# Batch 3's attention and token mixing two steps earlier in the first pair's second product

## The chip, the cores and the metric

The kernel runs on one core of a Trainium2 chip. The metric is the device time of one execution in microseconds (us). The engines are TensorE (PE, matmuls; PEld is its weight load), VectorE (DVE), ScalarE (ACT), GpSimd (POOL) and SyncE (SP, here only an issuer of DMAs). Each engine works through its own queue in order.

## The reference

Eight batches of attention (16 query heads, 4 key heads, 384 positions, 64 wide), followed by one ResMLP block over a model width of 1024:

```python
attn = softmax(q @ k.T / 8)                       # k, v repeated for groups of 4 query heads
x    = (attn @ v), heads side by side             # 8 x 384 x 1024
a1   = alpha1 * x + beta1
tok  = einsum('ts,bsd->btd', w_tok, a1)           # mixes the 384 positions
u    = x + lam * tok
a2   = alpha2 * u + beta2
ch   = maximum(a2 @ w_ch1, 0) @ w_ch2             # 1024 -> 4096 -> 1024
out  = u + lam * ch
```

## The kernel before

The two large products of the MLP set the pace. The batches are taken in four pairs. For each pair both products are done at once in a scheme with seven block products in place of eight, so that sums and differences of operands (`opb`, `tb`) and of weights (`w1`, and `w2` as blocks "11", "12", "21", "22") are formed on DVE beforehand. The first product of a pair gives the hidden layer, the second its output. While the products of one pair run, the attention and the token mixing of the next pair are done in between ("side work").

All five engines run in the order in which the program issues instructions. That order is written by hand: a pair's product is a generator that yields after each step, and a table `plan` says what is issued after which step. In the first pair's second product (`second_product`) a step is four C matmuls of 128x512 (L752), and there are 21 turns of 16 matmuls, 84 steps (0 to 83). After every turn ACT copies the sum out of its bank (L764) and, for turns 12 to 17, DVE adds a base (L767). Halfway through a turn ACT copies a start value into the bank of the next turn (L744). There are two such banks.

The side work of a batch (`side`) has 8 pieces p, one for each two query heads:

- `scores3`: three times four matmuls of scores (L260), each followed by an exponential on ACT (L269). Four exponential tiles go round.
- `av` (L295): 18 matmuls against v; then on DVE the reciprocal (L300), the scaling into `xr` (L303) and alpha1 (L309). `xr` and alpha1 are both in SBUF in L309; L303 reads PSUM.
- `tok` (L324, L328): the token mixing on PE; on DVE u = x + tok (L331, reads PSUM) and times alpha2 (L334, both inputs in SBUF), which gives the a2 of the piece. Then the piece's u is stored by SP (`spill`, 192 KB).
- `turn` (L398): three transposing matmuls of a2; ACT copies them (L400) into the operand for the next pair. In batch 2 a DMA transposes instead.

Each scores matmul group, `av`, `tok` and `turn` takes the next of three PSUM banks in rotation (`three`), and PE waits until what was in the bank three takes ago has been read.

Beside this, DVE works off the weights for later pairs: `sum_w2` (L499, 128x2048 bf16 with both inputs in SBUF; the results go to DRAM by SP, `keep_w2`) and `last_w2`, which is `sum_w2` with o = 4 at steps 61, 64, 68 and 71 for c = 0 to 3, and which frees a weight slot, so that POOL may issue the next load (`load_w1`, L183). From step 68 on a list `later` is flushed: POOL multiplies six finished tiles by lam (`scaled`, L790) and adds them to the output by DMA (L442).

At the end of the 84 steps come `sum_w1` (steps 77, 79 and 81, L510 and L515) and `sums_a` (L447 to L450), the sums of the next pair's operands. sums_a(j) needs the pieces j and j + 4 of batch 2 and j of batch 3. Then the next pair's first product begins (X, Y, Z at L831).

Batch 2's side work starts at step 0; its last pieces are `av` 7 at step 35 and `tok` 6 and 7 at steps 36 and 39. Batch 3's own table is shifted by 38.

Of the kernel before, what the change touches and what calls it, by code (L numbers as in the profile page):

```python
# [13 lines left out]
def kernel(  # L14
# [81 lines left out]
    turn, a2_turn = [0], [0]  # L96
# [117 lines left out]
    def side(b):  # L214
# [176 lines left out]
        def by_pe(p):  # L391
            return b in (0, 3) or b % 2 and p >= NP - (4 if first else 3)
# [14 lines left out]
        def put(k, *m):  # L407
            at.setdefault(k, []).append(m)
# [3 lines left out]
        for p in range(NP):  # L412
            put((4, 10, 14, 18, 24, 29, 33, 35)[p], av, p)
            put((8, 15, 17, 22, 27, 32, 36, 38 if b % 2 else 39)[p], tok_flip, p)
            if by_pe(p):
                put(((13, 20, 22, 28, 34, 37, 40, 42) if b == 3 else (0, 0, 0, 0, 0, 36, 39, 41))[p], turn, p)
        return at

    def loads(b):
# [147 lines left out]
    def free_blocks(side, gp):  # L567
        for kind in (side + "1", side + "2"):
            if (kind, gp) in block_slot:
                free(block_slot.pop((kind, gp)))  # L570
# [376 lines left out]
    with tc.manual_schedule(engines=order):  # L947
# [123 lines left out]
        def put(ps, phase, at, *m):  # L1071
            plan.setdefault((ps, phase, at), []).append(m)

        def put_all(ps, phase, table, at=lambda u: u):
            for u, ms in table.items():
                for m in ms:
                    put(ps, phase, at(u), *m)

        def put_flips(ps, phase, b, places):
            for u, m in zip(places, ((flip_k, b), *((flip_q, b, i, 2) for i in range(0, NP, 2)))):  # L1080
                put(ps, phase, u, *m)
# [30 lines left out]
        for ps in range(NB - 1):  # L1112
            c = 2 * ps + 2
            for i in range(9):
                put(ps, 0, (4, 8, 12, 16, 20, 24, 54, 58, 62)[i] if ps == 0 else 4 + 7 * i, load_next, c, 1)
                put(ps, 0, 70 + 3 * i if ps == 0 else 91 + 2 * i, load_next, c + 1, 1)
            put_flips(ps, 0, c, (44, 46, 50, 54, 58) if ps == 0 else range(76, 86, 2))
            put_all(ps, 1, side(c))
            for u, f, h in zip((8, 14, 14, 27, 32, 33) if ps == 0 else (10, 17, 18, 28, 33, 33),
                               (flip_q, flip_k, flip_q, flip_q, flip_k, flip_q), (0, 0, 2, 4, 2, 6)):  # L1120
                put(ps, 1, u, f, c + 1, h, 2)
            put_all(ps, 1, side(c + 1), lambda u: u + 38)
            for j, u in ((0, 77), (2, 80), (3, 83)) if ps == 0 else ((0, 76), (2, 79), (3, 81)):
                put(ps, 1, u, sums_a, j, 1 if j else 2)

        def steps(ps):
# [87 lines left out]
```

## Time and profile before

| what | value |
| --- | --- |
| three runs | 731.71, 734.32, 740.37 us; median 734.32 |
| the profiled execution | 731.92 us |
| its span | 729.9 us |
| PE busy | 717.4 us (98%) |
| DVE busy | 543.9 us (75%) |
| ACT busy | 373.8 us (51%) |
| POOL busy | 199.2 us (27%) |
| first pair's second product, first matmul to the next product's first | 128.1 to 234.4 us |

The span is the time between the first and the last instruction of the profiled execution; the execution's own time has 2.0 us more around it. A busy share is an average over the whole span. In the timelines a line gives the start in us from the span's start, the length in us, engine, line of the program, operation, output <- inputs, and how many instructions were merged; in brackets stands the idle time of the engine before it and what ended that.

### The profile page before, as it was taken

The page shows a single profiled execution, that of the slowest core. Times are in us where ns is not written, and L with a number is a line of the kernel's source. Part 1 is how long each engine was busy: PE and PEld are TensorE (multiplying, and loading weights), DVE is VectorE, ACT ScalarE, POOL GpSimd, SP SyncE. Part 2 cuts the span into 40 slices and gives each one's busy share as a digit, 9 for nine tenths or more (in the row PEclk, how much of TensorE's full clock was granted, in tenths as well). Part 3 has the DMA queues.
Part 4 walks back from the last instruction along what each step waited for, and adds up shares of the span by engine and source line. Part 5 has one row for each costly group of instructions (what it writes and reads, how often), then busy time and mean ns, then how long its engine had stood idle before and what let it go on. Part 6 is the DMA issues. An engine that isn't in the chain of part 4 may idle for free.

```text
span 729.9 us, 14511 instructions
## 1 busy us (share of the span) xinstructions
PE 717.4 (98%) x5716; PEld 408.7 (56%) x5716; DVE 543.9 (75%) x1009; ACT 373.8 (51%) x566; POOL 199.2 (27%) x242
## 2 busy tenths in 40 slices
PE   8899999999999999999999999999999999999998
PEld 4665555555555666555555566655555566654444
DVE  7888876577888988649678888748868988763354
ACT  7877666544563666643433466663333366650000
POOL 8844233221046551201022344200002222000011
PEclk9999999999999999999999999999999999999999
DMA  9999999999999999969989999998989999937965
GB/s 164 180 239 231 190 195 227 226 242 235 366 312 232 179 182 196 234 221 207 272 193 220 160 162 194 212 227 201 270 233 183 210 126 146 165 123 264 302 174 104
DMA packets 197616, 153.26 MB, mean 210 GB/s; under 512 B 90540, under 2 KB 175892, under 8 KB 197292
## 3 DMA queue, kind: packets, MB, share of 16 engines
q0 software_dynamic: 109872, 64.47, 65.4%
q1 hardware_dynamic: 86988, 87.42, 42.8%
q8 instruction: 44, 0.72, 0.4%
q10 hardware_dynamic: 688, 0.46, 0.2%
q14 instruction: 24, 0.20, 0.1%
HBM read 155.23 MB, written 39.85 MB: 267 GB/s over the span
## 4 chain that ended last, share of the span: by engine, by line
PE 90%; DVE 4%; POOL 2%; DMA 1%; issue 1%; ACT 1%; DVEq 0%; ACTq 0%; POOLq 0%
PE C L897 30%; PE X L831 17%; PE C L752 10%; PE Y L831 9%; PE Z L831 4%; PE sc L260 4%; PE X L681 4%; PE sc L295 3%; PE sc L324 3%; PE Y L681 3%; DMA ops<-obuf 1%; DVE pad L565 1%; PE Z L681 1%; PE tok L324 1%; POOL obuf L334 0%
## 5 line engine op out<-in xcount | busy, mean ns | idle before, releaser
L897 PE MATMUL C<-w,arena 128*128 128x512 bf16 (+2 forms) x744 | 168.3, 372 | 0.0
L269 ACT ACTIVATE es<-sc 128x1024 bf16<-128x1024 f32 x108 | 104.1, 1024 | 116.0 <-PE sc L260 107.6
L897 PEld LDWEIGHTS <-arena 128*128 128x128 bf16 x1040 | 94.8, 98 | 100.5 <-issue 5.1
L442 POOL DMA_DIRECT2D out_dram<-hT x45 | 40.0, 888 | 294.7 <-DVE hT L790 135.9
L836 ACT ACTIVATE hT<-X,bias 128x384 f32<-128x384 f32 x144 | 83.6, 582 | 60.0 <-PE X L831 55.2
L831 PEld LDWEIGHTS <-w 128*128 128x128 bf16 x768 | 75.1, 98 | 50.0
L831 PEld LDWEIGHTS <-pad 128*128 128x128 bf16 x576 | 56.4, 98 | 37.2
L183 POOL DMA_DIRECT2D w<-in_moe_w_ch_dram x48 | 45.4, 1002 | 105.6 <-PE X L831 36.5
L831 PE MATMUL X<-ops,w 128*128 128x384 bf16 x384 | 70.3, 326 | 0.0
L831 PE MATMUL X<-ops,pad 128*128 128x384 bf16 x384 | 70.3, 326 | 0.0
L897 PE MATMUL C<-pad,arena 128*128 128x512 bf16 (+2 forms) x296 | 70.2, 373 | 0.0
L324 PEld LDWEIGHTS <-wtokT 128*128 128x128 bf16 x576 | 39.0, 98 | 16.4 <-issue 3.4
L752 PEld LDWEIGHTS <-arena 128*128 128x128 bf16 x336 | 29.8, 98 | 30.0 <-issue 2.5
L331 DVE TENSOR_TENSOR xr<-sc,xr 128x384 f32<-128x384 f32 x48 | 26.5, 553 | 25.6 <-PE sc L324 14.3
L752 PE MATMUL C<-w,arena 128*128 128x512 bf16 x168 | 41.2, 379 | 0.0
L838 DVE TENSOR_TENSOR arena<-Y,hT 128x384 bf16<-128x384 f32 x48 | 26.5, 556 | 17.7 <-ACT hT L836 16.0
L295 PEld LDWEIGHTS <-es 128*128 128x128 bf16 x864 | 32.8, 97 | 11.3
L831 PE MATMUL Y<-ops,w 128*128 128x384 bf16 x192 | 39.1, 326 | 0.0
L831 PE MATMUL Z<-ops,w 128*128 128x384 bf16 x192 | 39.0, 326 | 0.0
L269 ACT ACTIVATE hT<-sc 128x1024 bf16<-128x1024 f32 x36 | 35.8, 1031 | 4.3 <-PE sc L260 4.0
L260 PE MATMUL sc<-qT,kT 64*128 64x384 bf16 (+2 forms) x504 | 37.2, 271 | 0.5 <-ACT hT L269 0.2
L842 ACT ACTIVATE arena<-X,bias 128x384 bf16<-128x384 f32 x48 | 27.9, 582 | 17.7 <-PE X L831 16.1
(190 smaller groups left out, 1175.1 us busy)
## 6 DMA issues: line engine op xcount, KB each, us to landing
w<-w2s SPq DMA_DIRECT2D x67, 512.0 KB, 5.1
w<-in_moe_w_ch_dram POOLq DMA_DIRECT2D x65, 512.0 KB, 9.8
pad<-w2s SPq DMA_DIRECT2D x25, 512.0 KB, 6.9
out_dram<-hT POOLq DMA_DIRECT2D x45, 256.0 KB, 7.1
out_dram<-xr SPq DMA_DIRECT2D x48, 192.0 KB, 5.3
q_raw<-in_q_dram POOLq DMA_DIRECT2D x28, 192.0 KB, 9.5
w2s<-w SPq DMA_DIRECT2D x10, 512.0 KB, 7.6
arena<-in_moe_w_ch_dram POOLq DMA_DIRECT2D x8, 512.0 KB, 15.9
```

What stands on the lines that cost most here:

```text
L183: nc.gpsimd.dma_start(out=w1[:, w1_slots[c]], in_=w1src[:, :, c * CW * P:(c + 1) * CW * P])
L260: nc.tensor.matmul(out=sc[:, hh, k % 4:k % 4 + n], lhsT=kT_[r, 2 * p // G, BLK[hh][sk], :], rhs=qT_[r, p, st:st + n, :], start=True, stop= ...
L269: nc.scalar.activation(out=e, in_=sc, func=EXP, scale=scale_qk)
L295: nc.tensor.matmul(out=av[:, hh, sq, :], lhsT=ess[k // 4][:, m % 2, k % 4, :], rhs=vb[:, sk, hk, :], start=(sk == 0), stop=(sk == NST - 1))
L324: nc.tensor.matmul(out=ps[:, tt, :], lhsT=wtokT[:, st, tt * P:(tt + 1) * P], rhs=a1s[p][:, st, :], start=(st == 0), stop=(st == NST - 1 an ...
L442: nc.gpsimd.dma_start(out=by_tok(out[b])[:, ms, dw * 512:(dw + 1) * 512], in_=o, accum_op=ADD)
L681: nc.tensor.matmul(out=ps[:, :n], lhsT=tb[G, o][:, dt, e * P:(e + 1) * P], rhs=opb(FIRST1[o], n)[:, dt], start=(o in (1, 2, 7) and dt == 0 ...
L752: nc.tensor.matmul(out=x, lhsT=lead_hid[:, t, FIRST2[o], ms * P:(ms + 1) * P], rhs=rhs[:, t % 4 * 512:(t % 4 + 1) * 512], start=(o in (1, ...
L831: nc.tensor.matmul(out=ps, lhsT=tb[g, o][:, dt, e * P:(e + 1) * P], rhs=opb(LEFT1[o])[:, dt], start=(o in (1, 2, 7) and dt == 0), stop=(dt ...
L836: nc.scalar.activation(out=snap[o, e], in_=ps, func=IDENT, bias=hi if o == 5 else lo)
L842: nc.scalar.activation(out=hid[:, t, 4], in_=ps, func=RELU, bias=hi)
L897: nc.tensor.matmul(out=x, lhsT=hid[:, t, LEFT2[o], ms * P:(ms + 1) * P], rhs=rhs[:, t % 4 * 512 + c0:t % 4 * 512 + c1], start=((not last o ...
```

## The change

It moves batch 3's whole side table from an offset of 38 to one of 36, for the first pair's second product alone (the later pairs keep 38). `turn` 2 of batch 3 goes from 22 to 23 in the table, so it moves from step 60 to 59, where all other pieces move by two. sums_a(0), for pieces 0 and 1, goes from step 77 to 76, ahead of the first sum_w1; sums_a(2) from 80 to 79; sums_a(3) from 83 to 81. The table of `turn` for batch 3 is not used elsewhere. No instruction is added or removed, and none has another shape.

```diff
             if by_pe(p):
-                put(((13, 20, 22, 28, 34, 37, 40, 42) if b == 3 else (0, 0, 0, 0, 0, 36, 39, 41))[p], turn, p)
+                put(((13, 20, 23, 28, 34, 37, 40, 42) if b == 3 else (0, 0, 0, 0, 0, 36, 39, 41))[p], turn, p)
...
-            put_all(ps, 1, side(c + 1), lambda u: u + 38)
-            for j, u in ((0, 77), (2, 80), (3, 83)) if ps == 0 else ((0, 76), (2, 79), (3, 81)):
+            put_all(ps, 1, side(c + 1), lambda u: u + (36 if ps == 0 else 38))
+            for j, u in ((0, 76), (2, 79), (3, 81)) if ps == 0 else ((0, 76), (2, 79), (3, 81)):
                 put(ps, 1, u, sums_a, j, 1 if j else 2)
```

Batch 3's steps, before and after:

| piece | before | after |
| --- | --- | --- |
| scores3 0 to 5 | 38, 44, 50, 59, 64, 69 | 36, 42, 48, 57, 62, 67 |
| av 0 to 7 | 42, 48, 52, 56, 62, 67, 71, 73 | 40, 46, 50, 54, 60, 65, 69, 71 |
| tok 0 to 7 | 46, 53, 55, 60, 65, 70, 74, 76 | 44, 51, 53, 58, 63, 68, 72, 74 |
| turn 0 to 7 | 51, 58, 60, 66, 72, 75, 78, 80 | 49, 56, 59, 64, 70, 73, 76, 78 |

## The prediction

> **What bounds the kernel now.** I read the page first, then windows of each engine's busy time over the first pair's second product, then the timelines of that stretch.
>
> The page: TensorE (PE) is busy for nearly all of the span.
>
> ```profile
> span 729.9 us, 14511 instructions
> PE 717.4 (98%) x5716; PEld 408.7 (56%) x5716; DVE 543.9 (75%) x1009; ACT 373.8 (51%) x566; POOL 199.2 (27%) x242
> ```
>
> The change removes no matmul, so it can win only idle time of PE. The windows show where that lies in the second product (127.9 to 234.5 us):
>
> ```profile
> 168.40:204.00 35.60, 35.60 (x348) 20.14 (x347) 27.69 (x44) 20.12 (x29) 0.91 (x1) 1.00 1.08 313
> 204.00:212.80 8.80, 8.21 (x82) 4.79 (x81) 7.64 (x12) 5.92 (x8) 1.76 (x2) 1.00 1.16 321
> 212.80:226.80 14.00, 12.81 (x138) 7.50 (x137) 12.65 (x16) 6.93 (x12) 12.44 (x11) 1.00 1.23 253
> ```
>
> Columns: stretch and its length, then PE, weight loads, DVE, ACT, POOL busy, granted clock (1.00), DMA share, GB/s. PE lacks 8.80 - 8.21 = 0.59 us in the second row and 14.00 - 12.81 = 1.19 us in the third, 1.78 us in all. That is 0.24% of the run: the most that can be won here. PE's timeline names the three places, in brackets at the line's end:
>
> ```profile
> 204.89 0.33 PE L324 MATMUL sc<-a,wtokT 128*128 128x128 bf16 x3 [0.59 <-ACT es L269]
> ...
> 221.20 0.33 PE L398 MATMUL sc<-ident,obuf 128*128 128x128 bf16 x3 [0.24 <-ACT es L269]
> ...
> 224.76 0.34 PE L324 MATMUL sc<-a,wtokT 128*128 128x128 bf16 x3 [0.95 <-DVE a L309]
> ```
>
> By the plan these are batch 3's tok 3 (step 60), turn 4 (step 72) and tok 6 (step 74). The first two wait for a score bank that an exponential still reads, the third for its operand from VectorE (DVE). Why DVE is late then is in its timeline and POOL's:
>
> ```profile
> 220.26 0.69 DVE L767 TENSOR_TENSOR hT<-C,hT 128x512 f32<-128x512 f32 x1 [0.39 <-ACT hT L764]
> 220.87 2.02 DVE L499 TENSOR_TENSOR w<-w,pad 128x2048 bf16<-128x2048 bf16 x1
> ...
> 223.62 1.08 DVE L309 TENSOR_TENSOR a<-xr,vecs 128x384 bf16<-128x384 f32 x1
> ...
> 225.44 1.74 DVE L309 TENSOR_TENSOR a<-xr,vecs 128x384 bf16<-128x384 f32 x1
> ```
>
> ```profile
> 211.92 0.88 POOL L183 DMA_DIRECT2D w<-in_moe_w_ch_dram  x1 [2.38 <-DVE pad L499]
> 212.82 1.28 POOL L790 TENSOR_TENSOR hT<-hT,vecs 128x512 f32<-128x512 f32 x1
> ...
> 220.24 1.55 POOL L790 TENSOR_TENSOR hT<-hT,vecs 128x512 f32<-128x512 f32 x1
> ...
> 222.71 1.57 POOL L790 TENSOR_TENSOR hT<-hT,vecs 128x512 f32<-128x512 f32 x1
> ...
> 225.19 1.56 POOL L790 TENSOR_TENSOR hT<-hT,vecs 128x512 f32<-128x512 f32 x1
> ```
>
> L499 otherwise takes 1.22 us and L309 0.56. Each slow one ends one ordinary length after a POOL L790 ends: 220.24 + 1.55 = 221.79, and 2.02 - 1.22 after 220.87 is 221.67; 222.71 + 1.57 = 224.28, and L309 ends at 224.70; 225.19 + 1.56 = 226.75, and the other L309 ends at 227.18. L331 and L303, with one input in PSUM, keep their 0.56 us there. So a DVE operation with both inputs in SBUF stands still while POOL multiplies. POOL's six multiplications start when the issue at 211.92 is through, every 2.5 us; that issue waits for the L499 of last_w2(1).
>
> The Trainium skill (SBUF — State Buffer, "Who interferes with whom") says the same as a rule: a DVE instruction with two SBUF inputs and a GpSimd instruction that reads SBUF exclude each other for the whole instruction, whoever starts first. Read as shared speed instead (2.02 / 1.22 = 1.7 times slower), the two collisions at the L499 and the L309 of av 7 below would cost about 0.8 + 0.4 us, not 1.7, and the sum would be 0.5 us less; the ends above speak for the rule.
>
> **The change, part by part.** I walked the queues of PE, ACT, DVE and POOL from step 32 (167.5 us) in the new order. Each instruction starts at the end of the one before it or at its last release. The lengths, start to start, are rows of the timelines: four C matmuls 0.86 us (0.96 after scores), score trio 0.76, av 0.55, tok 0.67, turn 0.17 on PE; exponential 0.91, L764 and L744 0.5 each, L400 0.37 on ACT; L300 0.22, L303 0.60, L309 0.47, L331 0.60, L334 0.48, L767 0.61, L499 1.14 on DVE; L790 1.28 and 0.96 for its store on POOL. The old order, walked alike, ends the product 0.4 us late (234.97 for 234.54) and gives the three stalls as 0.78, 0.41 and 1.50 us for 0.59, 0.24 and 0.95. So the walk finds the stalls, and is up to 0.6 us too harsh.
>
> *Moved by two steps: all 8 av, 8 tok, 7 turns and 18 scores of batch 3.* Their own time stays: 0 us. Each tok also issues one 192 KB store on SP. SP was behind anyway: tok 0 ran at 186.1 us, its store was issued at 195.5. The stores of tok 0, 2 and 4 pass one weight store each (steps 45, 54, 64), nothing else; the store that the L499 at 204.10 waits 1.1 us for keeps what is ahead of it. No moved step issues on POOL. 0 us; if a pass does delay that L499, it costs at most what the L499 has waited, 1.1 us.
>
> *Stall one.* tok 3 is now at step 58, one step after its scores, and turn 2 at 59 takes the next bank: four C matmuls lie between the three bank users. The walk leaves 0.12 of 0.59 us: **-0.5** (-0.6 to 0).
>
> *New at step 36.* Batch 2's tok 6 and batch 3's first scores now meet. The third score needs tok 6's own bank, free after its L331: the PE reaches it 0.50 us after tok, the bank is free 0.20 + 0.56 + 0.04 after: **+0.3** (0 to 0.6).
>
> *New at step 67.* The last score of the trio needs the bank of av 5 (step 65). DVE does av 5 only after last_w2(1) of step 64, to 215.1, and PE is there at 214.8: **+0.35** (0 to 1.0).
>
> *Stall two* (turn 4 behind the exponential of the score before it) keeps its order: 0 (-0.24 to 0.2).
>
> *Stall three, and what is late next.* What made tok 6 late hangs on C's steps, not on the side work: at step 71 L764, L767, then last_w2(3) (L499), and behind them the av of that step. In the old order that is av 6, which tok 6 needs at 74. In the new one it is av 7, which tok 7 needs at 74. tok 6 now has its av at 69 and runs at 72; the walk leaves 0.3 us of waiting: **-0.65** (-0.95 to 0.3). But tok 7 inherits the chain. From the end of step 71 PE has av 7, tok 6, turn 5 and three fours of C to cover it: 0.55 + 0.67 + 0.17 + 3 x 0.86 = 3.97 us. The chain needs L764 0.62, L767 0.61, L499 1.14, L300 0.22, L303 0.60, L309 0.56: 3.75 and some 0.2 for hand-overs. Alone it just fits. With POOL in it it doesn't. POOL's start moves too: last_w2(1) at step 64 now has tok 4's L331 and L334 ahead of it, and starts at 213.2 for 210.2. So POOL multiplies from 215.8 for 212.8, the third time from 220.5 to 221.8, the fourth from 222.8 to 224.1, the fifth from 225.0 (held up to 225.3) to 226.6. av 6's L309 comes at 220.9 and stands till 221.8, so L767 is 0.8 late; the L499 comes at 222.9, 0.1 behind POOL, and stands 1.2; av 7's L309 comes at 226.0 and stands 0.5. With 0.3 off, by which tok 6's own wait holds PE back, tok 7 waits 0.8 + 1.2 + 0.5 - 0.3 = **+2.2** (0 without a collision, 1.5 if the L499 goes ahead of POOL, 2.6 with multiplications of 1.5 us).
>
> *Operand sums sooner* (L1123, 77 to 76 and 83 to 81). In the walk DVE reaches them at 230.3 us (229.9 in the trace before), since it is behind: they only pass sum_w1. The last ends at 235.6, and the product at 235.9; Y's first matmul needs them 1.3 us later. 0 us. If that cover is gone, a late sum costs its lateness, at most some 0.6 us by the trace (L850's sum ends at 239.63, its matmul runs at 240.39).
>
> **Sum:** -0.5 + 0.3 + 0.35 + 0 - 0.65 + 2.2 = +1.7 us. The old order's walk was 0.4 us late, so from walk to walk it is +1.0 (235.93 less 234.97), and from the new walk to the trace's own end +1.4. I take the middle one, **+1.4 us**. The profiled execution took 731.92 us (span 729.9, 2.0 around it), so it would become 733.3. The three runs shown gave 731.71, 734.32 and 740.37; the middle of these four is 733.1, and with 1.4 **734.5 us**.
>
> **The rivals.**
>
> *A, tok 7 doesn't inherit (not slower).* DVE is on time at step 71. It decides there: av 6's L309 must be through by 221.2 us, so that L767 starts with its L764; the L499 then runs from 222.1, before POOL's fourth, and of the chain only L309 can stand, for 0.3. tok 7 then waits under 0.5 us, and -0.5 + 0.3 + 0.35 - 0.65 + 0.4 is -0.1 us; with the small new waits at their lower ends too it is -1.0. 732.6 us. For it: it asks 0.6 us of DVE, as much as the walk was too harsh at tok 6. Against it: in no phase of POOL that I tried (0.8 us earlier to 1.6 later) did the walk leave tok 7 less than 1.5.
>
> *B, DVE's lateness runs on.* Both collisions at full length and a third before tok 5 (the walk with POOL 0.8 us earlier and each multiplication 1.5 us): +3.8 us, 736.9 us. For it: L790 took 1.55 to 1.74 us in five of six cases. Against it: it needs all to fall together.
>
> *C, the edit is lost in the slack:* the waits that go and those that come are equal, as the sums gain nothing: 733.1 us, within 0.4. For it: the walk with POOL 0.8 us later gives 0.0.
>
> **How the numbers follow.** Forecast 0.50, A 0.20, B 0.12, C 0.18. Over POOL's phases the walks differ by -0.4 to +3.8 us; -1.8, with all three stalls gone and nothing new, is the floor. That is 731.3 to 736.9 on 733.1; the upper runs lie further out than the lower, so the range is 731.2 to 738.0. A measurement of this kernel can tell about 1% (7.3 us) from no change; no case reaches it. What is left is the scatter, 8.7 us between the fastest and slowest run: faster 0.04, same 0.87, slower 0.09.
>
> **What would show it.** Right: PE's wait at tok 3 is gone or under 0.2 us; a wait of 1 to 2.6 us for DVE L309 stands at batch 3's tok 7 (the last of L324's groups before the next product), with a slow L499 and L309 ahead of it beside an L790; the first L790 of the six starts some 3 us later; a few tenths at the scores after batch 2's tok 6. Wrong: no PE wait for L309 over 0.5 us in the last 15 us of the product; or a PE wait after it, at the first matmuls of X, Y or Z; or a change outside 128 to 240 us.

## The result: 0.7% slower, and the profile after

The changed kernel takes 737.81 us in the median of 21 runs, the kernel before 732.75 us: ratio 1.0066, interval [1.0044, 1.0087]. The profiled execution took 737.81 us with a span of 736.0 us. The loss lies in one place. From the first C matmul to the next product's first X matmul, the second product took 234.38 - 128.07 = 106.31 us before and 240.12 - 127.38 = 112.74 us after: +6.43 us, of a span that grew by 6.1.

The page and the windows of the last two stretches, with one more behind them (columns as in the prediction). The page counts two instructions more than before (14513 for 14511); the counts of all five engines are the same.

```profile
span 736.0 us, 14513 instructions
PE 720.0 (98%) x5716; PEld 409.0 (56%) x5716; DVE 546.2 (74%) x1009; ACT 373.8 (51%) x566; POOL 198.6 (27%) x242
```

```profile
204.00:212.80 8.80, 8.39 (x90) 4.70 (x89) 6.78 (x11) 5.72 (x9) 0.88 (x1) 1.00 1.18 313
212.80:226.80 14.00, 11.10 (x111) 6.02 (x110) 13.83 (x14) 5.81 (x9) 10.94 (x10) 1.00 1.21 258
226.80:236.00 9.20, 7.00 (x39) 3.63 (x38) 8.46 (x16) 1.92 (x4) 3.04 (x3) 0.81 0.88 196
```

In the last two rows PE idles 2.90 and 2.20 us (1.19 and nothing before), and in the last one the granted clock is 0.81 (1.00 before). DVE is busy for 13.83 of 14.00 us with only 14 instructions (16 before, in 12.65 us): busy here means standing. PE's timeline shows the waits at batch 3's tok 5, 6 and 7:

```profile
217.28 0.34 PE L324 MATMUL sc<-a,wtokT 128*128 128x128 bf16 x3 [1.08 <-DVE a L309]
...
224.78 0.34 PE L324 MATMUL sc<-a,wtokT 128*128 128x128 bf16 x3 [1.77 <-DVE a L309]
...
229.72 0.50 PE L324 MATMUL sc<-a,wtokT 128*128 128x128 bf16 x3 [2.21 <-DVE a L309]
...
230.97 2.94 PE L752 MATMUL C<-w,arena 128*128 128x512 bf16 x8
```

Three waits, 5.06 us in all, where the kernel before has one of 0.95. After the third the same matmuls are slower: the row of three takes 0.50 us (0.34 at tok 5 and 6), that of eight 2.94 (1.89 elsewhere). Windows of 2 us give the clock of that moment:

```profile
228.00:230.00 2.00, 0.28 (x3) 0.28 (x4) 1.96 (x3) 0.00 (x0) 1.70 (x2) 0.92 0.99 147
230.00:232.00 2.00, 2.00 (x15) 1.43 (x13) 1.44 (x4) 0.00 (x0) 0.41 (x1) 0.50 1.09 320
232.00:234.00 2.00, 2.00 (x11) 0.85 (x9) 1.97 (x5) 0.58 (x1) 0.00 (x0) 0.73 1.07 252
```

What the clock withheld is 0.08 x 2 + 0.50 x 2 + 0.27 x 2 = 1.70 us. The rows say much the same: from start to start tok 7 takes 1.25 us for 0.68, and the eight C matmuls 2.78 for 1.72, together 1.6 us more. DVE and POOL, in the order of time:

```profile
214.81 2.41 DVE L309 TENSOR_TENSOR a<-xr,vecs 128x384 bf16<-128x384 f32 x1
217.14 0.68 DVE L767 TENSOR_TENSOR hT<-C,hT 128x512 f32<-128x512 f32 x1
217.74 2.69 DVE L499 TENSOR_TENSOR w<-w,pad 128x2048 bf16<-128x2048 bf16 x1
...
220.93 1.33 DVE L334 TENSOR_TENSOR obuf<-xr,vecs 128x384 bf16<-128x384 f32 x1
...
223.00 1.73 DVE L309 TENSOR_TENSOR a<-xr,vecs 128x384 bf16<-128x384 f32 x1
224.64 0.68 DVE L767 TENSOR_TENSOR hT<-C,hT 128x512 f32<-128x512 f32 x1
225.24 2.62 DVE L499 TENSOR_TENSOR w<-w,pad 128x2048 bf16<-128x2048 bf16 x1
...
228.59 1.07 DVE L309 TENSOR_TENSOR a<-xr,vecs 128x384 bf16<-128x384 f32 x1
```

```profile
214.62 0.88 POOL L183 DMA_DIRECT2D w<-in_moe_w_ch_dram  x1 [3.49 <-PE sc L260]
215.52 1.28 POOL L790 TENSOR_TENSOR hT<-hT,vecs 128x512 f32<-128x512 f32 x1
217.10 0.94 POOL L442 DMA_DIRECT2D out_dram<-hT  x1 [0.30 <-POOL hT L790]
217.76 1.59 POOL L790 TENSOR_TENSOR hT<-hT,vecs 128x512 f32<-128x512 f32 x1
...
220.28 1.56 POOL L790 TENSOR_TENSOR hT<-hT,vecs 128x512 f32<-128x512 f32 x1
...
222.75 1.55 POOL L790 TENSOR_TENSOR hT<-hT,vecs 128x512 f32<-128x512 f32 x1
...
225.21 1.57 POOL L790 TENSOR_TENSOR hT<-hT,vecs 128x512 f32<-128x512 f32 x1
```

Each of these DVE operations with two SBUF inputs ends one ordinary length (0.56 us for L309 and L334, 1.22 for L499) after an L790 ends, to within 0.15 us. Then DVE does one or two operations that read PSUM (L767 takes 0.60 us from start to start), and comes with its next two-input operation just as the next L790 begins (217.74 against 217.76, 225.24 against 225.21) or up to 0.9 us into it. So six in a row stand for 1.85 + 1.47 + 0.77 + 1.17 + 1.40 + 0.51 = 7.2 us over their ordinary lengths. Before, five stood, for 1.21 + 0.37 + 0.80 + 0.52 + 1.18 = 4.1 us, and of these only the 0.80 + 0.52 lay ahead of a waiting matmul.

### The profile page after: what moved, and what is told of

It reads as the page before. It is cut to its first block, busy times and chain, and to the rows that moved or that the text cites. A ratio compares the mean times of both kernels' runs of the same rounds, so it can differ in the third digit from the quotient of the medians.

```text
span 736.0 us, 14513 instructions
## 1 busy us (share of the span) xinstructions
PE 720.0 (98%) x5716; PEld 409.0 (56%) x5716; DVE 546.2 (74%) x1009; ACT 373.8 (51%) x566; POOL 198.6 (27%) x242
## 4 chain that ended last, share of the span: by engine, by line
PE 83%; DVE 5%; POOL 4%; DMA 3%; issue 3%; ACT 1%; SPq 0%; POOLq 0%; DVEq 0%; ACTq 0%
PE C L897 30%; PE X L831 13%; PE C L752 8%; PE Y L831 7%; PE sc L260 4%; PE X L681 4%; PE sc L295 3%; PE Z L831 3%; PE sc L324 3%; PE Y L681 3%; DMA w<-in_moe_w_ch_dram 2%; PE E L613 1%; DMA w2s<-arena 1%; PE tok L324 1%; PE av L295 1%
## 5 line engine op out<-in xcount | busy, mean ns | idle before, releaser
L183 POOL DMA_DIRECT2D w<-in_moe_w_ch_dram x48 | 45.3, 1001 | 111.0 <-PE X L831 35.4
L324 PE MATMUL sc<-a,wtokT 128*128 128x128 bf16 x432 | 34.3, 221 | 5.2 <-DVE a L309 5.1
```

The lines of the kernel that those rows point to most:

```text
L183: nc.gpsimd.dma_start(out=w1[:, w1_slots[c]], in_=w1src[:, :, c * CW * P:(c + 1) * CW * P])
L324: nc.tensor.matmul(out=ps[:, tt, :], lhsT=wtokT[:, st, tt * P:(tt + 1) * P], rhs=a1s[p][:, st, :], start=(st == 0), stop=(st == NST - 1 an ...
```

## The experiments

Product lengths below are from the first C matmul to the first X matmul of one profiled execution. All medians stand against the kernel before in the same set of runs: 733.98 (first four), 733.85 (next four), 733.99 us (last four). The ratio is not the quotient of these medians; it is worked out from the runs of both kernels, and the two can differ by 0.15%.

### POOL's six multiplications left out, in both orders

```diff
-            if o != 2 or not last:
+            if (o != 2 or not last) and not (lead and o in (6, 7)):
```

The changed kernel:

> The changed kernel without POOL's multiplications by lam of the six tiles of turns 12 to 17 (they are stored unscaled). Theory 1: the three waits of PE for DVE L309 (1.08, 1.77 and 2.21 us at tok 5, 6 and 7) come from DVE standing still while POOL multiplies. Then all three fall under 0.5 us, the granted clock stays at 1.00 up to the end of the product, and the time is 731 to 733 us. Theory 2: DVE is late by its own load, that is by last_w2(3) put ahead of av 7 and by its 2.3 us of waiting for a weight store at 204 us; POOL is incidental. Then at least 3 of the 5.1 us of waiting stay and the time is over 736 us.

734.06 us, ratio 1.0013 [0.9991, 1.0034]; product 105.24 us, clock 1.00. None of the three waits is left. All DVE rows of the stretch are back at their ordinary lengths, for instance the last two operations ahead of tok 7, with last_w2(3) in front of av 7 as in the change:

```profile
229.77 1.21 DVE L499 TENSOR_TENSOR w<-w,pad 128x2048 bf16<-128x2048 bf16 x1
231.72 0.56 DVE L309 TENSOR_TENSOR a<-xr,vecs 128x384 bf16<-128x384 f32 x1
```

Theory 1 stands: without POOL's multiplications the whole loss is gone. DVE still waits 0.74 and 1.35 us for weight stores at 209 and 211 us in that run, and PE's only waits left in the product are 0.18 us at tok 3 and 0.26 at the scores of step 67. But the time is a little over the 731 to 733 expected; that is taken up below. The kernel before:

> The kernel before with the same six multiplications left out. Theory 1: the wait of 0.95 us at tok 6 goes, the two waits for an exponential (0.59 and 0.24 us) stay: 731.5 to 732.5 us against 732.75. Theory 2: all as before, 732.75 us. Beside the run without them in the new order it says what the new order is worth when POOL is out of the way: theory 1 says within 1 us of each other.

733.69 us, ratio 0.9999 [0.9973, 1.0025]; product 105.18 us. The wait at tok 6 went, the product is 1.1 us shorter, and the run isn't faster: 733.69 lies above the 731.5 to 732.5 expected.

### The multiplications let go earlier

```diff
-                    if t % 8 == 3 and later and (later[0][1] == 1 or k > 16 and later[0][1] != 4):
+                    if t % 8 == 3 and later and (later[0][1] == 1 or k > 12 and later[0][1] != 4):
```

> The changed kernel with the multiplications let go from turn 13 on (step 52) in place of turn 17 (step 68); nothing is left out. Theory 1: the first three run at 195 to 208 us, where DVE waits for stores anyway, and only the last three meet the end of batch 3's side work. The waits at tok 5 to 7 sum to 2.5 us at most for 5.1, and the time is 732.5 to 735 us. Theory 2: the waits stay as they are, 737 to 738 us.

733.98 us, ratio 0.9998 [0.9978, 1.0019]; product 107.35 us. Of the three waits 0.15 us is left (at tok 7), and 1.33 and 0.97 us of others came (tok 3, scores of step 67). The multiplications no longer follow in a train: the last three begin at 213.0, 217.8 and 223.6 us, so DVE gets through between them. DVE can come first, too: the L499 at 217.65 takes its 1.22 us, and the L790 at 217.82 takes 2.18. Nothing is left out here, so this is the whole loss undone by moving POOL's work alone.

> The kernel before with the multiplications let go from turn 13 on. Theory 1: the wait of 0.95 us at tok 6 falls under 0.5 us or moves to the sums at 194 to 206 us: 731.5 to 733 us against 732.75. Theory 2: 732.75 us.

733.35 us, ratio 0.9998 [0.9966, 1.0029]: no difference to be seen, 0.35 us above the range of theory 1. In the profiled execution, at 739.68 us the longest of the twelve, the wait at tok 6 is gone; others came in its place, the longest 1.93 us (C matmuls at 210.66, behind an L499 that had waited 3.64 us for a weight store and then stood 1.2) and 1.42 us (scores at 216.84, for L303), and the product took 110.60 us. So in this execution the waits moved more than they went.

### Which part of the change

```diff
@@ the kernel before, offset alone
-            put_all(ps, 1, side(c + 1), lambda u: u + 38)
+            put_all(ps, 1, side(c + 1), lambda u: u + (36 if ps == 0 else 38))
```

> The kernel before with the offset of 36 alone; turn 2 stays at 22 in the table (step 58) and the operand sums stay at 77, 80 and 83. Theory 1: the shift makes the loss; the waits at tok 5 to 7 are there, 737 to 738.5 us. Rival: the sums put ahead of sum_w1, or turn 2 moved apart from tok 3, make part of it: 733 to 736 us.

738.4 us, ratio 1.0066 [1.0042, 1.009]; product 113.19 us, with waits of 1.07, 1.78 and 2.21 us at the same three tok and a clock of 0.69 in the window of 232 to 236 us. So the offset alone makes a loss of the same size. The rest of the change, with the offset back at 38:

```diff
-            put_all(ps, 1, side(c + 1), lambda u: u + (36 if ps == 0 else 38))
+            put_all(ps, 1, side(c + 1), lambda u: u + 38)
```

> The changed kernel with the offset back at 38, so that only turn 2 one step later (61) and the earlier operand sums (76, 79, 81) are left of the change. Theory 1: within 0.7 us of the kernel before (732 to 734 us). Rival: over 735 us.

732.89 us, ratio 0.9995 [0.9972, 1.0018]; product 106.79 us. tok 6 waits 1.66 us for 0.95, the wait at tok 3 went; the time can't be told from that of the kernel before.

### What tok 7 waits for

last_w2(3) is moved behind av 7 within step 71:

```diff
-            put(0, 1, (61, 64, 68, 71)[c], last_w2, c)
+            put(0, 1, (61, 64, 68, 71)[c], last_w2, c) if c < 3 else None
...
                 put(ps, 1, u, sums_a, j, 1 if j else 2)
+            if ps == 0:
+                put(0, 1, 71, last_w2, 3)
```

> The changed kernel with last_w2(3) put after av 7 in step 71 in place of before it; nothing else. Theory 1 (tok 7 inherits what stood in front of tok 6, a weight difference held up by POOL): av 7's three operations no longer stand behind the L499 of 2.6 us, so the wait of 2.2 us at tok 7 falls under 0.6 us; the waits at tok 5 and tok 6 stay near 1.1 and 1.8 us; the granted clock stays higher at the end; 734.5 to 736.5 us against 737.8. Rival: DVE as a whole is late, the order within a step is of no matter; tok 7 keeps 1.5 us or more: 737 to 738 us.

735.78 us, ratio 1.0023 [0.9998, 1.0047]; product 108.72 us, clock 1.00. tok 5 waits 1.08 and tok 6 1.77 us as before, tok 7 not at all:

```profile
PE sc L324 <- DVE a L309: 2.8, 2, 1.8
```

(total us, times, longest.) So tok 7's 2.2 us did hang on the L499 put in front of its operand. The product is 4.0 us shorter for a wait of 2.2: without the third pause the clock doesn't fall in this execution either. In 11 of the 12 runs the mean granted clock is 0.999 or more; in the changed kernel that is so in 8 of 21.

### Idle matmuls in the waits

```diff
-            ps = bank([P, NST, P], "mm", "tok") if first else three()[:, 0, :NST]
+            if first:
+                ps = bank([P, NST, P], "mm", "tok")
+            else:
+                both = three()
+                ps = both[:, 0, :NST]
+                for _ in range((0, 0, 0, 0, 0, 5, 8, 10)[p] if b == 3 else 0):
+                    nc.tensor.matmul(out=both[:, 1].rearrange("p a b -> p (a b)")[:, :S], lhsT=wtokT[:, 0, :P],
+                                     rhs=wtokT[:, 1, :], start=True, stop=True)
```

> The changed kernel with 5, 8 and 10 idle matmuls of 384 columns (0.16 us each, 0.8, 1.3 and 1.6 us) put on PE right before batch 3's tok 5, 6 and 7, into the unused half of the bank; the output is not touched. They lie inside the waits of 1.1, 1.8 and 2.2 us. Theory (the pauses of PE bring its granted clock down, 0.50 was seen at 230 to 232 us, and that costs 1.6 us beside the waits): the clock stays at 1.00, tok 7 runs at full speed, and the time is 735.5 to 736.5 us. Rival (the lower clock is a matter of the runs, not of the pauses, or costs nothing): 737.5 to 738.5 us.

736.67 us, ratio 1.0038 [1.002, 1.0055]; product 111.46 us: 1.3 us less than in the changed kernel, with 23 matmuls more on PE.

```profile
226.80:236.00 9.20, 8.03 (x56) 4.34 (x55) 8.60 (x13) 2.48 (x5) 4.32 (x4) 1.00 1.03 224
```

The clock is 1.00 where the changed kernel had 0.81. Of the waits 0.26, 0.29 and 1.12 us are left, the last because the idle matmuls themselves wait there for their bank, so that tok 7 begins at 231.55 us, 0.5 us after its operand is ready (L309 ends at 230.96). So of the clock's 1.70 us some 1.2 are left to be won, and the product is 1.3 shorter. The median lies 0.17 us above the range expected, and the interval doesn't settle 1 us. The runs one by one say more: with the idle matmuls all 12 have a mean granted clock of 0.999 or more, and of the changed kernel only 8 of 21, with a median of 736.7 us; the 13 with 0.995 to 0.998 have one of 739.4. So the three waits don't bring the clock down in every run, but filling them kept it up in all 12. And where the clock stays up, the changed kernel loses 736.7 - 732.75 = 3.9 us, about as much as PE waits longer.

### The first collision

av 5's L309 stood from 214.81, though the row of the first L790 begins at 215.52. Here POOL must read a column of that L309's result before it multiplies:

```diff
+    hold = const.tile([P, 1], bf, tag="hold", name="hold")
...
+                if b == 3 and p == 5:
+                    nc.gpsimd.tensor_copy(out=hold, in_=a1s[p][:, 0, :1])
```

> The changed kernel with a copy of one column of av 5's L309 result put on POOL behind the load of step 64, so that POOL's six multiplications can't start before that L309 is through; nothing else. Theory (the first L790, which is ready behind the load's issue, keeps av 5's L309 standing from 214.8 us on, 0.7 us before L790's own row starts; the later collisions follow from the phase): that L309 takes 0.56 us for 2.40, the wait of 1.1 us at tok 5 goes; at least one of the waits at tok 6 and 7 (1.8 and 2.2 us) stays, as POOL goes on in the same rhythm: 734.5 to 737 us against 737.8. Rival (something else holds that L309): it keeps over 2 us, and the time is 737.5 us or more.

735.92 us, ratio 1.004 [1.0014, 1.0065]; product 108.49 us. av 5's L309 (now L310, the L790 L793):

```profile
217.02 0.56 DVE L310 TENSOR_TENSOR a<-xr,vecs 128x384 bf16<-128x384 f32 x1
217.49 0.68 DVE L770 TENSOR_TENSOR hT<-C,hT 128x512 f32<-128x512 f32 x1
218.09 2.12 DVE L502 TENSOR_TENSOR w<-w,pad 128x2048 bf16<-128x2048 bf16 x1
```

The load's issue lay beside this L309 as before (216.82 to 217.70 us), and alone it doesn't hold it. So it was the multiplication behind the issue that held it, from 0.7 us ahead of its own row on. tok 5's wait is gone, tok 6 waits 0.69 and tok 7 2.20 us: the next two-input operation (L502 here) falls into the rhythm again.

### Where the shorter product went

The runs without multiplications had products 1.1 us shorter than before and no gain. Their traces have a new wait right behind it (0.97 us in the new order, 1.70 in the old):

```profile
248.10 1.47 PE L831 MATMUL X<-ops,w 128*128 128x384 bf16 x8 [0.97 <-DVE ops L850]
```

L850 stands behind a weight difference (L515) that waits 6.17 us for a load (new order). It is put ahead of that:

```diff
-                if k == 3 and g == 0:
-                    tt(out=opb(6), in0=opb(4), in1=opb(5), op=SUB)
                 if k == 2 and g == 0:
                     sum_w1(0, 4)
+                    tt(out=opb(6), in0=opb(4), in1=opb(5), op=SUB)
```

> The changed kernel without the six multiplications (tiles stored unscaled), and with the next product's operand difference (L850) put ahead of the weight difference that waits for a load (L515). Without the multiplications the product was 1.1 us shorter than before, yet the run not faster, and its trace shows 1.0 us of waiting for L850 right behind. Theory: that wait gave the gain back; without it the time is 0.7 to 1.5 us less, 732.5 to 733.4 us for 734.06. Rival: the load itself bounds, PE waits a little later for the same load: 733.7 to 734.4 us.

733.26 us, ratio 1.0005 [0.9983, 1.0027].

> The kernel before without the six multiplications and with the same operand difference ahead. Its trace without the second edit has 1.7 us of waiting for L850. Theory: 731.8 to 732.8 us for 733.69. Rival as above: 733.3 to 734 us. If the new order with both edits is not faster than this one, the new order is worth nothing even with its collisions gone.

732.27 us, ratio 0.9964 [0.9932, 0.9996]. In both traces the wait for L850 is gone, and the longest that follows is 0.25 us; the medians fall by 0.8 and 1.4 us for waits of 1.0 and 1.7. Direction and size agree with the theory, but the intervals with and without the edit overlap, so it is not shown that this wait ate the gain. The new order isn't faster than the old one even so (733.26 against 732.27 us): with POOL and L850 out of the way no gain from it is to be seen.

> The changed kernel with the multiplications let go from turn 13 on and the operand difference ahead; nothing is left out. It stood at 733.98 without the second edit, and its trace had no wait for L850 but 2.3 us at tok 3 and at the scores of step 67. So the second edit brings little: 733 to 734 us, at most 0.3% under the kernel before.

732.97 us, ratio 1.0001 [0.9976, 1.0026]. No version that computes the whole reference beat the kernel before by more than its interval.

## Why the prediction was right or wrong

- **Direction and mechanism: right.** Slower, by DVE's lateness behind last_w2(3) and POOL, seen at tok 7, with the signs named beforehand. POOL's first multiplication was put at 215.8 us and came at 215.52 (the product itself began 0.69 us sooner, so against it 0.4 us late). The rule weighed there (SBUF — State Buffer, "Who interferes with whom", in the Trainium skill), that one side stands for the other's whole instruction, fits the lengths to 0.15 us; the reading as shared speed doesn't. Who starts first can't be read off the rows: the L309 at 214.81 began before the L790's row and stood all the same.
- **tok 7: the number is luck in part.** 2.2 us forecast, 2.21 measured, but two errors cancel in it. L767 came 2.37 us after its L764 had ended (222.27 to 224.64), where 0.8 was forecast; and tok 6's wait held PE back by 1.77 us, where 0.3 was taken off. The L499 and the L309 stood 1.40 and 0.51 us, as forecast (1.2 and 0.5).
- **Size: too small.** +1.4 us forecast, +5.1 in the medians, +6.4 in the product. On the profiled execution 733.3 was forecast and 737.81 came. The range of 731.2 to 738.0 held by 0.2 us, and only by what it had been widened for the scatter of runs: the harshest walk ended at 736.9. That it held is luck. And 1% was called the least that can be told from no change; the interval above tells 0.7%.
- **The term that failed most: tok 6** ("the walk leaves 0.3 us of waiting: -0.65"). It waits 1.77 us, +0.82 for -0.65. The walk had av 6's L309 stand 0.9 us for POOL (1.17 measured); but the L499 of last_w2(2) and tok 5's L334 ahead of it had stood 1.5 and 0.8 us too.
- **A term that was missing: tok 5**, 1.08 us. The walk let av 5's L309 (215.1 us) through because L790's row was to begin at 215.8. The rows came within 0.4 us of this; that a ready L790 holds the operation before its row begins was not in it. With that first collision all six fall into step. The walk with POOL 0.8 us earlier had shown a wait at tok 5, and I kept it for rival B, at 0.12. B was the nearest in mechanism, at +3.8.
- **A second missing term: the clock.** The walk took all matmuls at full speed; in the profiled execution the clock fell right after the pauses at tok 6 and tok 7 and cost 1.70 us. In 8 of 21 runs, with a mean granted clock of 1.000, it didn't fall.
- **Stall one: right.** tok 3 waits 0.18 us (0.12 forecast, 0.59 before).
- **Step 36 and step 67: right.** The score trios there take 1.11 and 1.06 us for 0.83: +0.28 and +0.23 (+0.3 and +0.35 forecast). A further 0.41 us came at the scores of step 62, for av 4's L303.
- **Stall two: within its bounds.** The wait at turn 4 (0.24 us) is gone; 0 (-0.24 to 0.2) was forecast.
- **Moved stores: put at 0, with a bound of 1.1 us.** The L499 that had waited 1.10 us for a store now waits 2.31 (204.40 us), and DVE works without a break from there to the L303 that the scores of step 62 wait 0.41 us for. Whether the passes on SP made that store later is not shown.
- **Operand sums sooner: right that they gain nothing.** They start at 232.3 us (229.9 before), and nothing waits for them.
- **The sum as measured:** 5.65 us of listed waits against 1.78 (+3.87), clock +1.70, trios +0.5, together 6.1 of 6.43 us; 0.4 is not assigned.

## What to carry to other kernels

Where two engines exclude each other, as here, a train of equal operations on one can force the other into its rhythm: each of its operations stands, and the next one comes just in time to stand again. So what counts is not how much the side work is moved but which operations it puts beside the train; moving the train (here to where DVE waits anyway) undid the loss without touching the side work. And a walk along the queues should be run over several phases, with the likeliest case taken from their spread: here it came out beyond the harshest phase tried (+5.1 us for +3.8).

## What the hardware showed that I had not expected

- POOL's hold begins before its row. Beside the issue of a load (L183, 214.62 to 215.50) a two-input L309 stood from 214.81 when an L790 was ready behind that issue. In the run with the early multiplications, an L309 at 216.58 beside the same kind of issue (216.43 to 217.35) took its 0.56 us; there the L790 behind it still waited for data. Why the hold begins so early is not shown, and neither is whether the row of the first L790 begins too late.
- Two pauses of PE of 1.77 and 2.21 us, 2.7 us of work apart, were followed by a granted clock of 0.50. By windows of 0.5 us it lasted 3.4 us (229.7 to 233.1), if the clock has only these two values there, and just as long in the run of the offset alone (231.1 to 234.5), where it began 0.7 us after the end of the third wait instead of with it. After pauses of 0.69 and 2.20 us (the first-collision run), or of 1.08 and 1.77 (last_w2(3) behind), the profiled executions show no such drop, nor do 8 of the 21 runs of the changed kernel. What decides is not shown. The Trainium skill (TensorE: Matmul & The Clock Gate, "Why this matters for your kernels") warns of gaps of over about 3 us; here the longest was 2.21 us.
- These waits repeat to 0.01 us from kernel to kernel (1.08, 1.77, 2.21 and 1.07, 1.78, 2.21), while whole runs scatter by 6 us and more.
